# Contiguous loads, 32x32 vector transposes and one Silu in a fused attention and MoE kernel

## The chip, the cores and the metric

The kernel runs on one core of one Trainium2 chip. The time is device microseconds (us) of that core. Engines are named as in the profile: PE is TensorE (matmuls), PEld its weight loads, DVE is VectorE, ACT is ScalarE, POOL is GpSimd, SP is SyncE, which here issues DMAs. A run is called slow when it is more than 1.5% above the fastest run of the same kernel. Most slow runs of this case go with a lower mean granted TensorE clock (not all: the slow run of `a_short` has 0.95, as two of its fast ones have), and comparisons here use fast runs only, unless said otherwise. The profile's span is about 2 us shorter than the device time of the same run.

## The reference

There are B=4 batches, H=4 heads, S=1088 tokens, D=32 and sketch rank r=8. Each row of q and k becomes 64 features, the products of 8 numbers `a` and 8 numbers `b`. The result of attention is the input x (4352 tokens by 128) of a mixture layer with 2048 hidden units.

```python
def phi(x):                                   # x: q or k, (4, 4, 1088, 32)
    a = einsum('rd,bhsd->bhsr', S1, x)        # 8 numbers a token
    b = einsum('rd,bhsd->bhsr', S2, x)        # 8 more
    return outer(a, b).reshape(..., 64)
kv  = einsum('bhsf,bhsd->bhfd', phi(k), v)
z   = phi(k).sum(axis=2)
num = einsum('bhsf,bhfd->bhsd', phi(q), kv)
den = einsum('bhsf,bhf->bhs', phi(q), z)[..., None] + 1e-6
x   = (num / den).transpose(0, 2, 1, 3).reshape(4352, 128)
h   = x @ w_in                                # 128 -> 2048
g   = h * sigmoid(beta * h)
out = g @ w_out                               # 2048 -> 128, float32
```

Both kernels fold beta into the weights (`winp = w_in * beta`, `woutp = w_out / beta`), so that g is a plain `h * sigmoid(h)`, which is Silu.

## The kernel before

Attention runs a batch at a time. Between its steps the program puts in "waves" of the mixture layer: a wave is two blocks of 128 hidden units for 512 tokens. The parts that matter here are these; cuts are marked.

```python
# loads: one DMA per head, in pieces of D*4 = 128 bytes; q, k on SP, v and weights on Pool
eng.dma_start(out=dst, in_=bass.AP(tensor=bh.tensor, offset=bh.offset,
                                   ap=[[D, P], [P * D, NSUB], [1, D]]))
# ... q4, k4 turned to qT4, kT4 by 128x128 fp32 transposes on PE, copied out by ACT ...

# a and b of q and k: abps -> abT; then a is spread to 64 rows by DMA:
nc.sync.dma_start(out=arep[64 * m : 64 * m + 64, :],
                  in_=bass.AP(tensor=asrc.tensor, offset=asrc.offset,
                              ap=[list(asrc.ap[0]), [0, R], [1, S]]))
# b is spread by a PE product with s2e, and phi(q) is their product on DVE:
nc.tensor.matmul(out=brep[:, :cw], lhsT=s2e[...], rhs=qT4[...], start=True, stop=True)
nc.vector.tensor_tensor(out=qp[...], in0=arep[...], in1=brep[:, :cw], op=mult)
# ... k: abT transposed (tkps), kp4all = a*b on DVE, transposed again (stage, kpt),
#     zcol = reduce_sum(kpt) on DVE, kvz = kp^T v on PE, assembled as ndb by ACT ...

# num and den in one PE product; the divide:
nc.scalar.activation(out=deps[...], in_=ndp[64:128, :cw], func=Identity, bias=epsb[...])
nc.vector.reciprocal(out=deps[:, :cw], in_=deps[:, :cw])
for pi in range(2):
    nc.vector.tensor_tensor(out=xT[...], in0=ndps[pi][0:64, :cw], in1=deps[...], op=mult)

# a wave: PE, then sigmoid on ACT, then a multiply on DVE that reads PSUM again
nc.scalar.activation(out=sig[:, :, :tw], in_=wave[:, :, :tw], func=Sigmoid)
nc.vector.tensor_tensor(out=gT[:, w0i : w0i + 2, :tw], in0=wave[:, :, :tw],
                        in1=sig[:, :, :tw], op=mult)
# ... end of a chunk: outT_ps over 16 blocks, copied by ACT, transposed on PE, copied, stored ...
```

Of the kernel before, what the change touches and what calls it, by code (L numbers as in the profile page):

```python
# [9 lines left out]
F16 = mybir.dt.float16  # L11

P = 128
# [3 lines left out]
def kernel(  # L17
# [20 lines left out]
    assert DM == H * D  # L38
    NP2 = 2

    s_sub = []
    o = 0
    while o < S:
        s_sub.append((o, min(P, S - o)))
        o += P
    NSUB = len(s_sub)
    s_chk = []
    o = 0
    while o < S:
        s_chk.append((o, min(512, S - o)))  # L50
        o += 512
    TCH = 512
    tok_chk = []
    o = 0
    while o < NTOK:
        tok_chk.append((o, min(TCH, NTOK - o)))
        o += TCH

    const = ctx.enter_context(tc.tile_pool(name="const", bufs=1))

    ident = const.tile([P, P], F32, tag="ident")
    make_identity(nc, ident)

    scat = const.tile([P, H * 2 * R], F32, tag="scat")
    nc.vector.memset(scat, 0.0)
    s2e = const.tile([P, P], F32, tag="s2e")
    nc.vector.memset(s2e, 0.0)
    with nc.allow_non_contiguous_dma(reason="tiny sketch-matrix transposes"):
        for h in range(H):
            nc.sync.dma_start(  # L70
                out=scat[32 * h : 32 * h + 32, 16 * h : 16 * h + 8],
                in_=S1.rearrange("r d -> d r"),
            )
            nc.sync.dma_start(
                out=scat[32 * h : 32 * h + 32, 16 * h + 8 : 16 * h + 16],
                in_=S2.rearrange("r d -> d r"),
            )
    for pi in range(NP2):
        for m in range(2):
            h = 2 * pi + m  # L80
            dst = s2e[64 * pi + 32 * m : 64 * pi + 32 * m + 32, 64 * m : 64 * m + 64]
            dst3 = bass.AP(tensor=dst.tensor, offset=dst.offset, ap=[[dst.ap[0][0], 32], [R, R], [1, R]])
            srcb = scat[32 * h : 32 * h + 32, 16 * h + 8 : 16 * h + 16]
            src3 = bass.AP(tensor=srcb.tensor, offset=srcb.offset, ap=[[srcb.ap[0][0], 32], [0, R], [1, R]])
            nc.vector.tensor_copy(out=dst3, in_=src3)

    xT = const.tile([P, NTOK], F16, tag="xT")
    epsb = const.tile([P, 1], F32, tag="epsb")
    nc.vector.memset(epsb, 1e-6)

    sbA = ctx.enter_context(tc.tile_pool(name="sbA", bufs=2))
    sbB = ctx.enter_context(tc.tile_pool(name="sbB", bufs=2))
    sbC = ctx.enter_context(tc.tile_pool(name="sbC", bufs=4))
    sbD = ctx.enter_context(tc.tile_pool(name="sbD", bufs=3))
# [4 lines left out]
    vcol = [0, 32, 65, 97]  # L99

    def load_batch(b):
        q4 = sbA.tile([P, NSUB, H, D], F32, tag="q4")
        k4 = sbA.tile([P, NSUB, H, D], F32, tag="k4")
        v4 = sbA.tile([P, NSUB, 130], F32, tag="v4")
        for h in range(H):
            for srcT, dst, eng in (
                (q, q4[:, :, h, :], nc.sync),
                (k, k4[:, :, h, :], nc.sync),
                (v, v4[:, :, vcol[h] : vcol[h] + D], nc.gpsimd),
            ):  # L110
                bh = srcT[b, h]
                if b == B - 1 and h == H - 1:
                    eng.dma_start(
                        out=dst[:, : NSUB - 1, :],
                        in_=bh[: (NSUB - 1) * P].rearrange("(t p) d -> p t d", p=P),
                    )
                    eng.dma_start(
                        out=dst[: S - (NSUB - 1) * P, NSUB - 1, :],
                        in_=bh[(NSUB - 1) * P :],
                    )  # L120
                else:
                    eng.dma_start(  # L122
                        out=dst,
                        in_=bass.AP(
                            tensor=bh.tensor,
                            offset=bh.offset,
                            ap=[[D, P], [P * D, NSUB], [1, D]],
                        ),
                    )
        nc.vector.memset(v4[:, :, 64:65], 1.0)  # L130
        nc.vector.memset(v4[:, :, 129:130], 1.0)
        return q4, k4, v4

    loaded = {0: load_batch(0)}
# [3 lines left out]
    NJH = NJ // 2  # L138
    if True:
        wstage = const  # L140
        beta_bc = wstage.tile([P, DFF], F32, tag="beta_bc")
        nc.gpsimd.dma_start(
            out=beta_bc,
            in_=bass.AP(tensor=moe_beta.tensor, offset=moe_beta.offset, ap=[[0, P], [1, DFF]]),
        )
        for half in range(2):
            w_in_sb = wstage.tile([P, DFF // 2], F32, tag="w_in_sb")
            nc.gpsimd.dma_start(out=w_in_sb, in_=moe_w_in[:, half * (DFF // 2) : (half + 1) * (DFF // 2)])
            nc.vector.tensor_tensor(
                out=winp[:, half * (DFF // 2) : (half + 1) * (DFF // 2)],  # L150
                in0=w_in_sb,
                in1=beta_bc[:, half * (DFF // 2) : (half + 1) * (DFF // 2)],
                op=mybir.AluOpType.mult,
            )
        betat = wstage.tile([P, NJ], F32, tag="betat")
        with nc.allow_non_contiguous_dma(reason="strided beta gather (one time)"):
            nc.sync.dma_start(out=betat, in_=moe_beta.rearrange("(j p) -> p j", p=P))
        rbetat = wstage.tile([P, NJ], F32, tag="rbetat")
        nc.vector.reciprocal(out=rbetat, in_=betat)
        for half in range(2):  # L160
            w_out_sb = wstage.tile([P, NJH, P], F32, tag="w_out_sb")
            nc.gpsimd.dma_start(
                out=w_out_sb,
                in_=moe_w_out[half * NJH * P : (half + 1) * NJH * P, :].rearrange("(j p) m -> p j m", p=P),
            )
            nc.vector.tensor_tensor(
                out=woutp[:, half * NJH : (half + 1) * NJH, :],
                in0=w_out_sb,
                in1=bass.AP(
                    tensor=rbetat.tensor,  # L170
                    offset=rbetat.offset + half * NJH,
                    ap=[[rbetat.ap[0][0], P], [1, NJH], [0, P]],
                ),
                op=mybir.AluOpType.mult,
            )

    moe_state = {"ci": 0, "w": 0, "gT": None, "ready_tokens": 0}

    def _moe_chunk_waves(ci, w0, nwaves):
        t0, tw = tok_chk[ci]  # L180
        gT = moe_state["gT"]
        for wi in range(nwaves):
            w0i = w0 + 2 * wi
            wave = psm.tile([P, 2, TCH], F32, tag="wave")
            for jj in range(2):
                jg = w0i + jj
                nc.tensor.matmul(  # L187
                    out=wave[:, jj, :tw],
                    lhsT=winp[:, jg * P : (jg + 1) * P],
                    rhs=xT[:, t0 : t0 + tw],  # L190
                    start=True,
                    stop=True,
                )
            sig = sbB.tile([P, 2, TCH], F16, tag="sig")
            nc.scalar.activation(  # L195
                out=sig[:, :, :tw],
                in_=wave[:, :, :tw],
                func=mybir.ActivationFunctionType.Sigmoid,
            )
            nc.vector.tensor_tensor(  # L200
                out=gT[:, w0i : w0i + 2, :tw],
                in0=wave[:, :, :tw],
                in1=sig[:, :, :tw],
                op=mybir.AluOpType.mult,
            )

    def _moe_chunk_tail(ci):
        t0, tw = tok_chk[ci]
        gT = moe_state["gT"]
        outT_ps = pso.tile([P, TCH], F32, tag="moeout")  # L210
        for j in range(NJ):
            nc.tensor.matmul(  # L212
                out=outT_ps[:, :tw],
                lhsT=woutp[:, j, :],
                rhs=gT[:, j, :tw],
                start=(j == 0),
                stop=(j == NJ - 1),
            )
        outT_sb = sbB.tile([P, TCH], F32, tag="outT_sb")
        nc.scalar.copy(out=outT_sb[:, :tw], in_=outT_ps[:, :tw])  # L220
        nsubt = (tw + P - 1) // P
        out_sb = sbB.tile([P, TCH // P, P], F32, tag="out_sb")
        otok = pso.tile([P, TCH], F32, tag="moeout")
        for u in range(nsubt):
            uw = min(P, tw - u * P)
            nc.tensor.matmul(
                out=otok[:uw, u * P : u * P + P],
                lhsT=outT_sb[:, u * P : u * P + uw],
                rhs=ident,
# [232 lines left out]
```

## Time and profile before

The median of the first three runs was 311.13 us (308.25 to 314.45). The table divides the span by the ends of the last xT write of a batch, which is where a batch of attention is finished.

| stretch of the span (310.9 us) | us | what runs |
|---|---|---|
| start to the end of batch 0 | 96.3 | attention alone |
| batches 1 to 3 | 180.0 | attention with waves between its steps |
| the tail | 34.6 | waves alone |

These lines are from the page of the kernel before: busy time by engine, the busy tenths of PE and the granted TensorE clock in 40 equal slices, the DMA packets, and the chain of work that ended last by engine.

```profile
PE 198.6 (64%) x790; PEld 105.6 (34%) x790; DVE 161.6 (52%) x204; ACT 127.5 (41%) x216; POOL 20.8 (7%) x28
...
PE   0007302698559929994696499668927995686762
...
PEclk9999855555557967998779579975985899789998
...
DMA packets 48939, 17.04 MB, mean 55 GB/s; under 512 B 42144, under 2 KB 46752, under 8 KB 48800
...
PE 38%; DVE 19%; DMA 15%; SPq 14%; ACT 9%; issue 3%; ACTq 0%; DVEq 0%
```

No engine is full, and PE does almost nothing in the first three slices. The chain spends 29% of the span on DMA transfers and on SP issuing them. The next lines are the costly groups of the same page. After the bar stand the busy time and the mean ns of one; after the second bar stand the idle time just before them and what ended most of it.

```profile
L200 DVE TENSOR_TENSOR gT<-wave,sig 128x1024 f16<-128x1024 f32 (+1 forms) x72 | 81.9, 1154 | 38.9 <-ACT sig L195 38.5
L195 ACT ACTIVATE sig<-wave 128x1024 f16<-128x1024 f32 (+1 forms) x72 | 69.2, 978 | 46.4 <-PE wave L187 43.5
...
L321 DVE TENSOR_TENSOR qp<-arep,brep 128x512 f32<-128x512 f32 (+1 forms) x24 | 11.3, 527 | 46.7 <-DMA arep<-abT 46.7
L419 DVE RECIPROCAL deps<-deps 128x512 f32<-128x512 f32 (+1 forms) x12 | 29.0, 2413 | 7.9 <-ACT deps L412 7.9
```

The multiply of the waves takes half of DVE's work, and phi(q) waited 46.7 us for the DMA that spreads a. Whether such waits count is seen in the chain of waits, in order of time (start, length, what):

```profile
45.12 12.25 DMA arep<-abT
60.49 3.12 PE stage L370 x9
63.61 4.22 PE kvz L384 x18
...
102.79 11.36 DMA arep<-abT
```

They count: the arep copy is on the chain in every batch, for 12.25 us in the first and about 11.4 us in each other. The ACT and DVE timeline of the tail shows why a wave is slow when nothing else runs:

```profile
278.64 2.16 ACT L195 ACTIVATE sig<-wave 128x1024 f16<-128x1024 f32 x2 [0.98 <-PE wave L187]
...
279.70 2.36 DVE L200 TENSOR_TENSOR gT<-wave,sig 128x1024 f16<-128x1024 f32 x2 [0.61 <-ACT sig L195]
...
281.60 2.16 ACT L195 ACTIVATE sig<-wave 128x1024 f16<-128x1024 f32 x2 [0.81 <-PE wave L187]
```

A pair of waves comes every 281.60 - 278.64 = 2.96 us. The wave's PSUM buffer is held by sigmoid and then by the multiply, so ACT idles 0.8 to 1 us in each pair.

### The profile page before, as it was taken

To read this page: it belongs to the slowest core of one execution; us is meant where nothing else is said; L and a number is where in the kernel's file an instruction comes from. 1 tells how busy PE (TensorE), PEld (TensorE's weight loads), DVE (VectorE), ACT (ScalarE), POOL (GpSimd) and SP (SyncE) were. 2 spreads that over 40 slices of the span, in tenths; PEclk is the share of its full clock that TensorE was granted. 3 is DMA by queue.
4 is the path that set the end of the run, shared out by engine and by line. 5 is a ranking of instruction groups with operands and counts; after the bars stand their busy time and mean duration, and the time that the engine had idled before them with its cause. 6 is when DMAs were issued, how large, how long until landed. Compare 5 with 4: busy or idle time off the path is not lost.

```text
span 310.9 us, 2305 instructions
## 1 busy us (share of the span) xinstructions
PE 198.6 (64%) x790; PEld 105.6 (34%) x790; DVE 161.6 (52%) x204; ACT 127.5 (41%) x216; POOL 20.8 (7%) x28
## 2 busy tenths in 40 slices
PE   0007302698559929994696499668927995686762
PEld 0005101386125314641442148225403571242231
DVE  1003301421676336858933376786325849887862
ACT  1003000132157415572563064735630755377762
POOL 8202200004100000050000000000000000000000
PEclk9999855555557967998779579975985899789998
DMA  4999954811203745030104410001142100010110
GB/s 74 296 146 122 219 71 91 124 17 30 47 0 50 81 82 103 13 75 0 34 2 54 82 41 2 0 0 34 16 61 67 37 0 0 0 34 2 34 34 18
DMA packets 48939, 17.04 MB, mean 55 GB/s; under 512 B 42144, under 2 KB 46752, under 8 KB 48800
## 3 DMA queue, kind: packets, MB, share of 16 engines
q1 hardware_dynamic: 42672, 9.18, 21.6%
q0 software_dynamic: 1760, 5.50, 6.7%
q10 hardware_dynamic: 4496, 2.23, 2.6%
q8 instruction: 6, 0.10, 0.1%
q14 instruction: 5, 0.04, 0.0%
HBM read 10.22 MB, written 2.23 MB: 40 GB/s over the span
## 4 chain that ended last, share of the span: by engine, by line
PE 38%; DVE 19%; DMA 15%; SPq 14%; ACT 9%; issue 3%; ACTq 0%; DVEq 0%
DMA arep<-abT 15%; SPq L122 10%; DVE gT L200 9%; DVE deps L419 9%; PE kvz L384 7%; PE wave L187 6%; PE ndp L405 5%; ACT sig L195 5%; PE stage L370 5%; PE outT_ps L212 4%; PE brep L314 4%; PE stage L274 3%; SPq L303 2%; PE abps L289 2%; ACT deps L412 2%
## 5 line engine op out<-in xcount | busy, mean ns | idle before, releaser
L200 DVE TENSOR_TENSOR gT<-wave,sig 128x1024 f16<-128x1024 f32 (+1 forms) x72 | 81.9, 1154 | 38.9 <-ACT sig L195 38.5
L195 ACT ACTIVATE sig<-wave 128x1024 f16<-128x1024 f32 (+1 forms) x72 | 69.2, 978 | 46.4 <-PE wave L187 43.5
L187 PE MATMUL wave<-xT,winp 128*128 128x512 f16 (+1 forms) x144 | 50.5, 426 | 21.3 <-DVE gT L200 20.5
L212 PE MATMUL outT_ps<-gT,woutp 128*128 128x512 f16 (+1 forms) x144 | 46.1, 408 | 13.3 <-DVE gT L200 12.1
L321 DVE TENSOR_TENSOR qp<-arep,brep 128x512 f32<-128x512 f32 (+1 forms) x24 | 11.3, 527 | 46.7 <-DMA arep<-abT 46.7
L419 DVE RECIPROCAL deps<-deps 128x512 f32<-128x512 f32 (+1 forms) x12 | 29.0, 2413 | 7.9 <-ACT deps L412 7.9
L405 PE MATMUL ndp<-qp,ndb 128*128 128x512 f32 (+1 forms) x48 | 26.3, 675 | 5.6 <-DVE xT L421 3.9
L187 PEld LDWEIGHTS <-winp 128*128 128x128 f16 x144 | 16.1, 114 | 31.6 <-issue 24.9
L412 ACT ACTIVATE deps<-ndp,epsb 64x512 f32<-64x512 f32 (+1 forms) x24 | 13.4, 559 | 30.1 <-PE ndp L405 29.9
L212 PEld LDWEIGHTS <-woutp 128*128 128x128 f16 x144 | 14.9, 106 | 27.2 <-issue 17.6
L405 PEld LDWEIGHTS ndp<-qp,ndb 128*128 128x128 f32 x48 | 11.2, 261 | 34.5 <-DVE xT L421 18.1
L274 PE MATMUL stage<-ident,q_103 128*128 128x128 f32 (+1 forms) x9 | 2.2, 418 | 25.3 <-DMA q_103<-in_q_dram 25.3
L314 PE MATMUL brep<-qT_157,s2e 64*128 64x512 f32 (+1 forms) x12 | 6.2, 672 | 18.5 <-DVE qp L321 18.5
L370 PE MATMUL stage<-ident,kp4all 128*128 128x128 f32 (+1 forms) x72 | 16.2, 324 | 1.2 <-DVE kp4all L360 1.0
L381 DVE TENSOR_REDUCE zcol<-kpt 128x1 f32<-128x1088 f32 x8 | 10.2, 1279 | 11.1 <-ACT kpt L379 11.1
L345 ACT COPY tkS<-tkps 128x512 f32<-128x512 f32 (+1 forms) x8 | 2.9, 400 | 28.2 <-PE tkps L335 28.1
L360 DVE TENSOR_TENSOR kp4all<-tkS 128x256 f32<-128x256 f32 (+1 forms) x36 | 12.4, 417 | 1.8 <-ACT tkS L345 1.8
L370 PEld LDWEIGHTS stage<-ident,kp4all 128*128 128x128 f32 (+1 forms) x72 | 10.0, 155 | 8.3 <-DVE kp4all L360 5.8
L421 DVE TENSOR_TENSOR xT<-ndp,deps 64x512 f16<-64x512 f32 (+1 forms) x24 | 12.5, 523 | 0.5
L379 ACT COPY kpt<-stage 128x512 f32<-128x512 f32 (+1 forms) x24 | 10.3, 463 | 5.2 <-PE stage L370 5.0
L220 ACT COPY outT_sb<-outT_ps 128x512 f32<-128x512 f32 (+1 forms) x9 | 5.0, 560 | 17.7 <-PE outT_ps L212 17.7
L283 ACT COPY qT_157<-stage 128x512 f32<-128x512 f32 (+1 forms) x3 | 1.3, 463 | 24.7 <-PE stage L274 24.7
(96 smaller groups left out, 199.5 us busy)
## 6 DMA issues: line engine op xcount, KB each, us to landing
arep<-abT SPq DMA_DIRECT2D x16, 272.0 KB
out_dram<-out_sb ACTq DMA_DIRECT2D x8, 256.0 KB, 2.3
beta_bc<-in_moe_beta_dram POOLq DMA_DIRECT2D x1, 1024.0 KB, 9.0
w_in_sb<-in_moe_w_in_dram POOLq DMA_DIRECT2D x2, 512.0 KB, 7.8
w_out_sb<-in_moe_w_out_dram POOLq DMA_DIRECT2D x2, 512.0 KB, 9.4
q_103<-in_q_dram SPq DMA_DIRECT2D x4, 144.0 KB
v_105<-in_v_dram POOLq DMA_DIRECT2D x4, 144.0 KB, 5.1
k_104<-in_k_dram SPq DMA_DIRECT2D x4, 144.0 KB, 11.9
```

The source lines that it names most:

```text
L122: eng.dma_start(out=dst, in_=bass.AP(tensor=bh.tensor, offset=bh.offset, ap=[[D, P], [P * D, NSUB], [1, D]],),)
L187: nc.tensor.matmul(out=wave[:, jj, :tw], lhsT=winp[:, jg * P : (jg + 1) * P], rhs=xT[:, t0 : t0 + tw], start=True, stop=True,)
L195: nc.scalar.activation(out=sig[:, :, :tw], in_=wave[:, :, :tw], func=mybir.ActivationFunctionType.Sigmoid,)
L200: nc.vector.tensor_tensor(out=gT[:, w0i : w0i + 2, :tw], in0=wave[:, :, :tw], in1=sig[:, :, :tw], op=mybir.AluOpType.mult,)
L212: nc.tensor.matmul(out=outT_ps[:, :tw], lhsT=woutp[:, j, :], rhs=gT[:, j, :tw], start=(j == 0), stop=(j == NJ - 1),)
L314: nc.tensor.matmul(out=brep[:, :cw], lhsT=s2e[64 * pi : 64 * pi + 64, :], rhs=qT4[64 * pi : 64 * pi + 64, c0 : c0 + cw], start=True, stop= ...
L370: nc.tensor.matmul(out=stage[:, gi * P : gi * P + sw], lhsT=kp4[g0 + gi][:sw, pi * P : (pi + 1) * P], rhs=ident[:sw, :sw], is_transpose=Tr ...
L384: nc.tensor.matmul(out=kvz[:, 0:65], lhsT=kp4[st][:sw, pi * P : (pi + 1) * P], rhs=v4[:sw, st, pi * 65 : pi * 65 + 65], start=(st == 0), s ...
L405: nc.tensor.matmul(out=ndp[:, :cw], lhsT=ndblk[pi], rhs=qpT[pi][:, c0 : c0 + cw], start=True, stop=True,)
L412: nc.scalar.activation(out=deps[64 * pi : 64 * pi + 64, :cw], in_=ndp[64:128, :cw], func=mybir.ActivationFunctionType.Identity, bias=epsb[ ...
L419: nc.vector.reciprocal(out=deps[:, :cw], in_=deps[:, :cw])
L421: nc.vector.tensor_tensor(out=xT[64 * pi : 64 * pi + 64, b * S + c0 : b * S + c0 + cw], in0=ndps[pi][0:64, :cw], in1=deps[64 * pi : 64 * p ...
```

## The change

The intent is to shorten every one of these stages: load q and k in runs of 34 tokens (4352 bytes), turn them with DVE transposes of 32x32 blocks instead of PE transposes, spread a by a PE product instead of a DMA, compute k's features already transposed for the kv sums in 32-column tiles of PE, divide num by den in one 128-row operation, replace sigmoid and multiply by one Silu, and transpose the output straight out of PSUM. The token order inside a head is permuted by the loads, and the stores undo it. The core of the diff, with cuts:

```diff
-    eng.dma_start(out=dst, in_=bass.AP(..., ap=[[D, P], [P * D, NSUB], [1, D]]))   # per head; v on Pool
+    nc.sync.dma_start(out=t, in_=bass.AP(tensor=src.tensor, offset=src[b, 0].offset,
+                                         ap=[[T * D, P], [1, T * D]]))    # a whole batch, T = 34
+    # order on SP: k0, v0, q0, w_in, w_out, then k, v, q of batches 1 to 3; S1, S2, beta on ACT
-    # PE transposes into `stage`, ACT copies to qT4, kT4
+    nc.vector.transpose(out=kT, in_=k_t[b].rearrange("p t d -> p (t d)"))
+    # a and b of k, by 32x32 tiles, then turned out of PSUM:
+    nc.tensor.matmul(out=kps[32 * g : 32 * g + 32, : NJK * 32], lhsT=sw[rows, :], rhs=kT[...])
+    nc.vector.transpose(out=kab[:, h]..., in_=kps[:, : NJK * 32])
+    # kp = a*b: heads 0, 1 on DVE, heads 2, 3 on Pool
-    nc.sync.dma_start(out=arep[64 * m : 64 * m + 64, :], in_=...)          # spread a by DMA
+    nc.tensor.matmul(out=aps[:, :cw], lhsT=sa[rows, :], rhs=qT[rows, c0 : c0 + cw])
+    nc.scalar.copy(out=asb[pi][:, :cw], in_=aps[:, :cw])                   # spread a by PE
-    # kpt transposes, reduce_sum zcol, kvz of 18 matmuls
+    for n, j in enumerate([1, 2, 3, 4, 5, 6, 7, 8, 0]):                    # kv and z sums
+        for which in range(2):
+            for h in range(H):
+                nc.tensor.matmul(out=kvz[32 * h : 32 * h + 32, F * which : F * which + F],
+                                 lhsT=v_t[b][:kr, h, j, :] if which == 0 else ones[:kr, :],
+                                 rhs=kp[:kr, h, j, :], ...)
-    for pi in range(NP2): nc.vector.tensor_tensor(out=xT[64 * pi ...], ...)
+    nc.vector.tensor_tensor(out=xT[:, ...], in0=num[:, :cw], in1=deps[:, :cw], op=MUL)
-    nc.scalar.activation(out=sig, in_=wave, func=Sigmoid)
-    nc.vector.tensor_tensor(out=gT, in0=wave, in1=sig, op=mult)
+    nc.scalar.activation(out=g, in_=wv, func=ACTF.Silu)
-    # ACT copy, PE transposes, ACT copy, store
+    nc.vector.transpose(out=o_sb..., in_=moe["acc"][:, :tw])               # then store, 128-byte pieces
+    # beta is spread by PE (ones_row x beta_row -> bb) instead of a broadcast DMA
+    for b in range(B):
+        steps = attention(b)
+        if b == 0:
+            next(steps)
+            next(steps)
+            prep_weights()
+        for _ in steps:
+            pump(2)                       # two waves after each of the nine steps, where ready
```

## The prediction

> **What bounds the kernel now.** No engine is full: the profile's first part has PE 64%, DVE 52%, ACT 41%. Time goes in three stretches (chain of waits and a table of stretches). (a) 0 to 92 us: one batch of attention alone. PE first works at 25.3 us, because q and k arrive as 128-byte pieces (42,144 of 48,939 packets are under 512 B; the chain gives 10% to issuing those loads); the arep copies hold qp from 45 to 57 us; then PE runs at a granted clock of 0.5. (b) 92 to 272 us: three batches of about 60 us, each with an 11.4 us wait of qp for arep (46.7 us of waits in all) and the long chain of kp transposes, zcol, kvz and ndb. (c) 272 to 311 us: MoE alone. A wave is read by both sigmoid (1.03 us) and the DVE multiply (1.21 us), so with two wave buffers a pair of waves takes 2.96 us (timeline).
>
> **What changes.**
> - ACT: 72 Sigmoids become 68 Silus. I take 1.03 us each: the Trainium skill, "ScalarE: Activation LUTs" (step-by-step section), says one element per cycle whatever the function; the trace's 1026 and 598 ns for 1024 and 512 elements fit that rate. Out and q/k evictions go. Estimate: 127 to about 93 us.
> - DVE: 82 us of gT multiplies go; 33 transposes of estimated 0.45 to 1.3 us come (about 23 us). The reciprocal keeps its 29 us (6.3 ns an element, from 3348 and 544 ns), xT halves. 162 to about 85 us.
> - PE: about 90 fp32 transposes go; kps, doubled a/b products and 288 small kvz matmuls come. fp32 costs 0.85 us per 512 columns at full clock, double at half (the same six brep records took 2.15 us at 31 us and 4.10 at 52 us). Column tiles do overlap here: the two abps matmuls start within 10 ns. This agrees with the skill's "TensorE: Matmul & The Clock Gate", Part 3. So per batch I estimate kps 2.5, a/b 6, kvz 7 (144 passes near 50 ns, the shakiest term), num/den 4: 20 us, plus 16 waves at 0.86 us = 14: 34 us, the fullest engine.
> - DMA: arep (4.4 MB) and the beta broadcast vanish; q/k/v load in long runs. Output is now in 128-byte pieces, but off the chain until the last.
>
> **Sum.** First kps near 8 us instead of 25. Batch 0 ends at about 44 us (w_in landing, partly a cold clock, three 3.1 us reciprocal/xT steps); three batches of about 41 us (PE 34 plus stalls: three PSUM banks let the reciprocal chain of about 9 us hold num/den and, in program order, the waves behind them); then 20 waves left, ACT-bound at 1.05, 21 us, plus 4 for the last transpose and store: 44 + 123 + 25 = 192 us. Nearly all of the 119 us gain lies on the chain: about 48 from the start, 57 from the batches, 14 from the tail.
>
> I predict 192 us, 8 in 10 between 170 and 218; faster by over 2% 0.98, within 2% 0.01, slower 0.01.
>
> **What would show it.** First PE work at 7 to 12 us; no arep waits; Silu mean near 1.03 us; tail spacing about 1.05 us a wave with ACT over 90% there; stretches of about 41 us between the batches' last xT writes; PE the busiest engine; deps reciprocal the longest DVE group.
>
> **What would make it wrong.** kvz passes not overlapping or paying more for weight loads or tile changes (over 12 us a batch); a half clock throughout attention (plus 30 us); Pool products (kp, woutp) slow enough to hold kvz; evictions queued behind Silu on ACT making PE wait. Faster if a/b row pairs overlap and the clock stays full (170).

## The result

The changed kernel gives the right output. Its median is 182.31 us over four runs (181.04 to 188.35), beside 310.2 us for the kernel before in the same rounds (308.25 to 314.45). One run of each was slow. The ratio of the fast runs is 0.5875, with a 95% interval of 0.5835 to 0.5916. A ratio here is always the mean time of one kernel's fast runs over that of the other's of the same rounds, so it is not quite the ratio of the medians quoted. A later control of the unchanged new kernel on another chip (`a_again`, below) gave 182.3 us.

| stretch | before | after | predicted |
|---|---|---|---|
| start to the end of batch 0 | 96.3 | 44.7 | 44 |
| batches 1 to 3 | 180.0 | 112.1 | 123 |
| tail | 34.6 | 23.4 | 25 |
| sum | 310.9 | 180.2 | 192 |

So 51.6 us of the gain lie in the start, 67.9 in the batches and 11.2 in the tail. The same lines of the page as before:

```profile
PE 147.1 (82%) x1201; PEld 59.9 (33%) x1201; DVE 82.0 (45%) x113; ACT 88.9 (49%) x122; POOL 15.0 (8%) x17
...
PE   0079996849999998399999977999999738988870
...
PEclk9999999699999999969999999999999995799998
...
DMA packets 22480, 11.35 MB, mean 63 GB/s; under 512 B 18738, under 2 KB 20802, under 8 KB 22338
...
PE 68%; ACT 9%; DVE 9%; issue 7%; DMA 4%; ACTq 0%; SPq 0%; DVEq 0%
```

PE now starts in the third slice and holds 68% of the chain; DMA and its issue have fallen from 29% to 4%. The groups that answer to those shown before:

```profile
L228 ACT ACTIVATE g<-wave 128x1024 f16<-128x1024 f32 x68 | 66.2, 1021 | 28.9 <-PE wave L220 28.7
...
L359 DVE RECIPROCAL deps<-deps 128x384 f32<-128x384 f32 (+1 forms) x12 | 28.4, 2395 | 7.0 <-ACT deps L358 7.0
...
L304 DVE TENSOR_TENSOR qp<-bps,asb 128x384 f32<-128x384 f32 (+1 forms) x24 | 12.4, 533 | 30.2 <-PE bps L301 30.0
```

A Silu of 1024 elements took 1021 ns and the sigmoid that it replaces 1026 ns. This agrees with the Trainium skill, "ScalarE: Activation LUTs", section "Step-by-step: what each stage is for", which says that the throughput is one element per cycle and lane whatever the function, measured there as 0.833 ns an element. Here the difference between sigmoids of 1024 and 512 elements gives (1026 - 598) / 512 = 0.836 ns.

The reciprocal kept its cost (28.4 us against 29.0). The idle time before phi(q) is still 30 us, but it is now waiting for PE, the fullest engine, and is no cost in itself.

The table of stretches of the changed kernel (window, its length, busy time and instructions of PE, PEld, DVE, ACT and POOL, then granted clock, DMA share, GB/s), for the start from 10 us on, the three batches, and the tail:

```profile
10.00:44.70 34.70, 29.34 (x248) 13.18 (x225) 25.10 (x31) 9.66 (x22) 6.43 (x3) 0.95 0.69 202
44.70:82.00 37.30, 33.24 (x297) 12.72 (x296) 19.26 (x26) 19.84 (x27) 2.73 (x2) 0.95 0.10 15
82.00:119.00 37.00, 34.97 (x302) 13.46 (x299) 17.63 (x25) 22.68 (x30) 2.31 (x2) 1.00 0.10 15
119.00:156.00 37.00, 32.32 (x275) 12.26 (x274) 15.52 (x20) 18.91 (x27) 2.31 (x2) 0.91 0.10 16
156.00:180.20 24.20, 16.84 (x85) 8.04 (x84) 2.38 (x4) 16.18 (x17) 0.00 (x0) 0.98 0.18 28
```

PE is busy for 33.24 of 37.3 us in the first batch, 34.97 and 32.32 of 37.0 in the next two. In the tail's timeline, ACT is the limit:

```profile
159.49 1.94 ACT L228 ACTIVATE g<-wave 128x1024 f16<-128x1024 f32 x2 [0.26 <-PE wave L220]
161.68 1.94 ACT L228 ACTIVATE g<-wave 128x1024 f16<-128x1024 f32 x2 [0.26 <-PE wave L220]
```

A pair of waves now comes every 161.68 - 159.49 = 2.19 us, 1.10 us a wave instead of 1.48, and ACT idles 0.26 us of each pair.

### The profile page after: what moved, and what is told of

The parts are those of the page before. It is cut to its first block, busy times and chain, and to the rows that moved or that the text cites. A ratio compares the mean times of both kernels' runs of the same rounds, so it can differ in the third digit from the quotient of the medians.

```text
span 180.2 us, 2944 instructions
## 1 busy us (share of the span) xinstructions
PE 147.1 (82%) x1201; PEld 59.9 (33%) x1201; DVE 82.0 (45%) x113; ACT 88.9 (49%) x122; POOL 15.0 (8%) x17
## 2 busy tenths in 40 slices
DMA packets 22480, 11.35 MB, mean 63 GB/s; under 512 B 18738, under 2 KB 20802, under 8 KB 22338
## 4 chain that ended last, share of the span: by engine, by line
PE 68%; ACT 9%; DVE 9%; issue 7%; DMA 4%; ACTq 0%; SPq 0%; DVEq 0%
PE wave L220 17%; PE moeout L180 16%; PE aps L293 10%; ACT g L228 7%; PE kvz L314 6%; PE bps L301 5%; PE kps L261 5%; DVE deps L359 4%; PE bb L152 4%; PE num L350 3%; DMA v<-in_v_dram 3%; PE den L350 2%; DMA sraw<-in_S_dram 1%; ACT deps L358 1%; DVE xT L360 1%
## 5 line engine op out<-in xcount | busy, mean ns | idle before, releaser
L228 ACT ACTIVATE g<-wave 128x1024 f16<-128x1024 f32 x68 | 66.2, 1021 | 28.9 <-PE wave L220 28.7
L180 PE MATMUL moeout<-g,woutp 128*128 128x512 f16 (+1 forms) x144 | 41.9, 375 | 4.0 <-ACT g L228 4.0
L359 DVE RECIPROCAL deps<-deps 128x384 f32<-128x384 f32 (+1 forms) x12 | 28.4, 2395 | 7.0 <-ACT deps L358 7.0
L304 DVE TENSOR_TENSOR qp<-bps,asb 128x384 f32<-128x384 f32 (+1 forms) x24 | 12.4, 533 | 30.2 <-PE bps L301 30.0
L293 PE MATMUL aps<-qT,sa 64*128 64x384 f32 (+1 forms) x48 | 22.0, 581 | 0.1
L180 PEld LDWEIGHTS <-woutp 128*128 128x128 f16 x144 | 12.1, 98 | 26.7 <-issue 17.7
L297 ACT COPY asb<-aps 128x384 f32<-128x384 f32 (+1 forms) x24 | 11.2, 465 | 17.6 <-PE aps L293 12.8
L277 POOL TENSOR_TENSOR kp<-kab 128x576 f32<-128x576 f32 x8 | 10.2, 1291 | 105.8 <-DVE kab L268 105.8
L350 PE MATMUL num<-qp,nd 128*64 128x384 f32 (+1 forms) x48 | 13.8, 535 | 5.7 <-DVE xT L360 5.7
L301 PE MATMUL bps<-qT,sb 64*128 64x384 f32 (+1 forms) x48 | 16.5, 544 | 0.0
L350 PE MATMUL den<-qp,nd 128*64 128x384 f32 (+1 forms) x48 | 10.7, 525 | 1.3 <-DVE nd L343 1.2
```

The source lines that it names most:

```text
L180: nc.tensor.matmul(out=moe["acc"][:, :tw], lhsT=woutp[:, j, :], rhs=g[:, jj, :tw], start=(j == 0), stop=(j == NJ - 1),)
L228: nc.scalar.activation(out=g, in_=wv, func=ACTF.Silu)
L277: eng.tensor_tensor(out=kp[:, h].rearrange("p j (i l) -> p j i l", i=R), in0=bass.AP(tensor=a0.tensor, offset=a0.offset, ap=[pst, [32, NJK ...
L293: nc.tensor.matmul(out=aps[:, :cw], lhsT=sa[rows, :], rhs=qT[rows, c0 : c0 + cw], start=True, stop=True)
L297: nc.scalar.copy(out=asb[pi][:, :cw], in_=aps[:, :cw])
L301: nc.tensor.matmul(out=bps[:, :cw], lhsT=sb[rows, :], rhs=qT[rows, c0 : c0 + cw], start=True, stop=True)
```

## The experiments

Twelve kernels ran. The first four build parts of the change into the kernel before, to see what each is worth there. The rest take parts out of the changed kernel, or change one thing in it. The theories were these. Theory A (the prediction): the gain comes from removing chain items one by one (late loads, arep, DVE multiply), and what is left is bound by PE in the batches. Its rivals: one single item explains most of it; the piece size of the loads explains the start; PE is not the limit, but the reciprocal's chain is.

The stretches of the runs that the argument uses, from their profiles, cut as above (all of fast runs):

| kernel | start to end of batch 0 | batches 1 to 3 | tail | span |
|---|---|---|---|---|
| before | 96.3 | 180.0 | 34.6 | 310.9 |
| `b_silu` | 96.1 | 165.4 | 20.9 | 282.4 |
| `b_aps` | 78.1 | 145.7 | 45.6 | 269.4 |
| `b_aps_silu` | 77.2 | 125.6 | 22.3 | 225.1 |
| `b_order` | 68.3 | 125.6 | 22.8 | 216.6 |
| after | 44.7 | 112.1 | 23.4 | 180.2 |
| `a_kvz` | 51.2 | 130.5 | 23.4 | 205.1 |
| `a_f16ab` | 43.4 | 96.5 | 23.4 | 163.3 |
| `a_pump` | 44.9 | 97.9 | 24.9 | 167.7 |
| `a_final` | 40.3 | 97.6 | 24.9 | 162.8 |

### Silu alone in the kernel before: `b_silu`

```diff
-            nc.scalar.activation(out=sig[:, :, :tw], in_=wave[:, :, :tw], func=Sigmoid)
-            nc.vector.tensor_tensor(out=gT[...], in0=wave[:, :, :tw], in1=sig[:, :, :tw], op=mult)
+            nc.scalar.activation(out=gT[...], in_=wave[:, :, :tw], func=Silu)
```

> The kernel before with Silu written straight to gT, no DVE multiply. Theory (the gain comes from the chain: load pieces, arep copies and the long attention chain; the MoE counts only in the tail): the tail of 39 us falls by about 10, each 60 us batch by at most 3, so 290 to 300 us. Rival (the costliest group, the 82 us gT multiply on DVE, was what bounded the kernel): at most 245 us.

Measured: 283.5 us (282.4 to 285.0), ratio 0.916 (0.910 to 0.922), a gain of about 26.5 us. That is more than the theory allowed (290 to 300 us) and far less than the rival asked (245 us or less). DVE's busy time fell from 161.6 to 83.3 us, so only a third of the 78 us taken from DVE came off the time. The list of waits of this run says where the rest went (who waited for what, us in total, times, longest):

```profile
DVE qp L314 <- DMA arep<-abT: 89.8, 8, 18.6
```

DVE now arrives earlier at phi(q) and waits there for the arep DMA, 89.8 us instead of 46.7. The gain is 13.7 us in the tail, where waves run alone, and 14.6 in the batches.

### The spread of a by PE alone, in the kernel before: `b_aps`

```diff
-                nc.sync.dma_start(out=arep[64 * m : 64 * m + 64, :], in_=bass.AP(... [0, R] ...))
+            for c0, cw in s_chk:
+                aps = ps.tile([P, 512], F32, tag="bank")
+                nc.tensor.matmul(out=aps[:, :cw], lhsT=s1e[64 * pi : 64 * pi + 64, :],
+                                 rhs=qT4[64 * pi : 64 * pi + 64, c0 : c0 + cw], start=True, stop=True)
+                nc.scalar.copy(out=arep[:, c0 : c0 + cw], in_=aps[:, :cw])
```

> The kernel before with arep made by a PE product and an ACT copy instead of the DMA copies. Theory: the 46.7 us of waits for arep go, some 2 to 4 us of PE work per batch comes, 262 to 278 us. Rival (DVE multiply the bound): at least 300 us, since the multiplies would fill the time.

Measured: 271.1 us (270.6 to 271.8), ratio 0.876 (0.871 to 0.881), a gain of 39 us, less than the 46.7 us of waits removed. The start and the batches gained 18.2 and 34.3 us, but the tail grew by 11 us. The table of stretches for this tail:

```profile
224.00:269.40 45.40, 29.33 (x130) 12.59 (x128) 30.93 (x29) 28.48 (x36) 0.00 (x0) 0.95 0.07 20
```

28 sigmoids start after the last batch here, and 21 in the kernel before: attention now ends sooner, and the waves, which still need sigmoid and multiply, have not kept up.

### Both together: `b_aps_silu`

The edit is the sum of the two above.

> Both single changes in the kernel before. Theory: gains add, 245 to 265 us, and the rest of the way to 182 is the loads, transposes and kp/kvz chain. Rival: with the arep wait gone the DVE multiply matters far more than alone: 215 us or less.

Measured: 227.15 us (226.8 to 228.3), ratio 0.7345 (0.730 to 0.739), a gain of 83 us. The two gains alone sum to 26.5 + 39 = 65.5, so together they give about 17 us more. Neither expectation was met: the gains do not just add (245 to 265 us), and the rival's 215 us was not reached. In the profiles the excess is 85.8 - 28.5 - 41.5 = 15.8 us, and the stretches place it: 9.6 us in the tail (which grew by 11.0 with the PE spread alone and shrinks by 12.3 with both), 5.5 in the batches, 0.7 in the start. Each fix alone ran into the wait that the other removes. The table of stretches over the three batches, first of the kernel before, then of this one, shows the same from the side of PE:

```profile
96.70:276.30 179.60, 135.86 (x561) 70.77 (x559) 110.20 (x129) 88.23 (x152) 4.48 (x5) 0.83 0.21 36
```

```profile
77.20:202.80 125.60, 118.87 (x594) 65.10 (x593) 57.74 (x83) 92.23 (x170) 4.46 (x5) 1.00 0.13 27
```

PE is now busy for 118.87 of 125.6 us, and its granted clock in this stretch rose from 0.83 to 1.00. Two of the many edits, neither touching transposes or loads, explain 83 of the 128 us.

### The order of the loads: `b_order`

`b_aps_silu` with all loads on the one SP queue in the order of need; the pieces stay 128 bytes. Each half of w_in and w_out also gets a tile of its own, so that no load waits for a tile to come free.

```diff
-                (v, v4[:, :, vcol[h] : vcol[h] + D], nc.gpsimd),
+                (v, v4[:, :, vcol[h] : vcol[h] + D], nc.sync),
-        nc.gpsimd.dma_start(out=beta_bc, ...)      # w_in, w_out likewise
+        nc.sync.dma_start(out=beta_bc, ...)        # after q, k, v of batch 0
```

> The kernel before with both single changes (arep on PE, Silu), and all loads on one queue in the order of need: sketch matrices, q, k, v of batch 0, then the weights, then batch 1. The pieces stay 128 bytes. Theory (competition: 3 MB of weights and v on a second queue held back q and k, more than the piece size did): first PE work at 13 to 18 us instead of 25, 212 to 221 us. Rival (the number of small pieces, among them 4-byte ones for the sketch matrices, sets the start): first PE work after 22 us, 227 us within 2%.

Measured: 219.01 us (218.4 to 220.6), ratio 0.703 (0.696 to 0.710). The control of the changed kernel ran on the same chip:

> The changed kernel, unaltered, on the same chip and rounds as the next one: 182 us within 1%.

It gave 182.3 us (182.1 to 183.2), ratio 0.585. The PE timeline shows the first PE work, first in the kernel before, then in `b_order`:

```profile
25.30 1.94 PE L274 MATMUL stage<-ident,q_103 128*128 128x128 f32 x8 [25.30 <-DMA q_103<-in_q_dram]
```

```profile
16.87 2.23 PE L274 MATMUL stage<-ident,q 128*128 128x128 f32 x9 [16.87 <-DMA q<-in_q_dram]
```

PE starts 8.4 us sooner with pieces of the same size (`b_aps_silu`, the direct neighbour, starts at 25.38 us, as late as the kernel before), and the whole kernel gains about 8 us, all in the start (77.2 to 68.3). So the loads on the second queue (v, the weights and beta) had been holding q and k back. This agrees with the Trainium skill, "DMA: Bandwidth & Descriptors", section "Queues, rings and completion order", which says that each DMA engine serves the queues that have work in turn. Which of the moved loads did the harm, and whether the second queue or only the order mattered, was not separated. It was not the number of short pieces: packets under 512 B even rose, from 42,016 to 60,384.

### The piece size of the loads, undone in the changed kernel: `a_short`

```diff
-        t = ld.tile([P, T, D], F32, tag=tag, name=tag)
+        t = ld.tile([P, T, D + 8], F32, tag=tag, name=tag)      # padded rows: no long runs
-            out=t, in_=bass.AP(..., ap=[[T * D, P], [1, T * D]]))
+            out=t[:, :, :D], in_=bass.AP(..., ap=[[T * D, P], [D, T], [1, D]]))
```

> The changed kernel with k and q loaded in 128-byte pieces (same tiles, padded rows), all else kept. Theory (short pieces are what delayed the first PE work, 25.3 us before against 9.6 after): the first kps comes 4 to 12 us later, later batches do not care, 186 to 196 us. Rival (the earlier start comes from the order of the loads and the missing arep, not the piece size): within 2% of 182.

Measured: median 184.5 us, fast runs 183.2 to 184.6, ratio 0.593 (0.590 to 0.596), beside 181.9 us for the mean of the changed kernel's fast runs in its own rounds. Packets under 512 B rose from 18,738 to 53,554, and the transpose of k started at 6.73 us instead of 5.35. So short pieces cost 1.4 us at the first load and about 2 us in all. The expectation of 4 to 12 us was wrong. Little of the time hung on the piece size: the first PE work waits for the turned sketch matrices, and it moved only from 9.64 to 10.25 us. The DVE and PE timelines of `a_short`:

```profile
6.73 1.31 DVE L254 STREAM_TRANSPOSE kT<-k 128x1088 f32<-128x1088 f32 x1 [5.38 <-DMA k<-in_k_dram]
```

```profile
10.25 1.25 PE L261 MATMUL kps<-kT,sw 32*32 32x288 f32 x24 [10.25 <-DVE sw L119]
```

### Sigmoid and multiply put back: `a_sigmoid`

```diff
-        nc.scalar.activation(out=g, in_=wv, func=ACTF.Silu)
+        sig = sbG.tile([P, 2 * TCH], F16, tag="sig", name="sig", bufs=2)
+        nc.scalar.activation(out=sig, in_=wv, func=ACTF.Sigmoid)
+        nc.vector.tensor_tensor(out=g, in0=wv, in1=sig, op=MUL)
```

> The changed kernel with Sigmoid and a DVE multiply in place of Silu. Theory: the tail grows by about 9 us (a pair of waves back to about 2.96 us), the batches from 37 to about 43 because DVE then has 40 us of work each: 205 to 220 us. Rival (Silu is most of the gain): 245 us or more.

Measured: one fast run of 202.94 us; three others (206.6 to 210.1), with the profiled one among them, count as slow, so no ratio was formed. The fast run lies 2 us below the expected 205 to 220. Fast against fast, Silu is worth about 202.9 - 181.9 = 21 us in the changed kernel. With a single fast run this is a rough number. In the kernel before it was 26.5 alone and, on top of the PE spread, 271.1 - 227.15 = 44. The worth of one edit depends on what else is in place.

### The order of heads in the kv sums: `a_kvz`

The matmuls are the same in number and shape, but the loop over heads is outermost, so that neighbours write to the same 32 output rows of PSUM, that is, to the same column tile of PE.

```diff
-        for n, j in enumerate([1, 2, 3, 4, 5, 6, 7, 8, 0]):
-            kr = 64 if j == 0 else P
-            for which in range(2):
-                for h in range(H):
+        for h in range(H):
+            for n, j in enumerate([1, 2, 3, 4, 5, 6, 7, 8, 0]):
+                kr = 64 if j == 0 else P
+                for which in range(2):
```

> The changed kernel with the loop over heads outside in kvz, so that neighbouring small matmuls use the same 32-column tile. Theory (column tiles overlap, which is why kvz took 2.2 us and not the 7 of the prediction): kvz 6 to 9 us a batch, 195 to 208 us in all. Rival (a pass costs its 16 ns of issue wherever it goes): kvz stays near 2.2 us, 182 us.

Measured: 208.84 us (207.2 to 210.1), ratio 0.674 (0.670 to 0.679), about 27 us slower. From the chain of waits, first the changed kernel, then `a_kvz` (start, length, what):

```profile
27.84 2.37 PE kvz L314 x144
...
63.94 2.16 PE kvz L314 x134
```

```profile
27.72 8.98 PE kvz L314 x144
...
70.43 8.74 PE kvz L314 x140
```

A record (each fp32 matmul leaves two) takes 8.74 / 140 = 62 ns in this order and 2.16 / 134 = 16 ns when the four heads alternate, about four times less. The product takes 6 to 9 us, as the theory expected; the total is a little above its 195 to 208. The difference of 6.6 us a batch, four times, is 26.4 us, which is about the whole loss. The PE timeline of the changed kernel shows the same from closer by (start, time from first start to last end, group):

```profile
27.82 0.32 PE L314 MATMUL kvz<-kp,v 128*32 128x64 f32 x8
27.95 0.29 PE L314 MATMUL kvz<-kp,ones 128*32 128x64 f32 x8
```

A group of eight records lasts about 0.3 us, and the next group starts 0.12 to 0.13 us after it began. This agrees with the Trainium skill, "TensorE: Matmul & The Clock Gate", Part 3 ("Packing small matmuls"), which says that matmuls in different tiles of the array run at the same time and start about 4 ns apart. The 4 ns are not shown here: the trace gives 16 ns a record on average. The new order also changes which weights follow each other and which rows of PSUM are written in turn; no run separates these from the column tile.

### a and b of q in half precision: `a_f16ab`

Its output is wrong, which doesn't matter for the time. `sa`, `sb` and a copy of qT made on Pool are float16, so the 96 records of those products become 48.

```diff
-    sa = const.tile([P, P], F32, tag="sa")      # sb likewise
+    sa = const.tile([P, P], F16, tag="sa")
+        nc.gpsimd.tensor_copy(out=qTh, in_=qT)  # qTh float16, used as rhs of aps and bps
```

> The changed kernel with the a and b products in float16 (qT cast on the idle Pool; the result may be off, and is only to show time). Theory (PE bounds the batches): PE loses 5 us or more a batch, 160 to 168 us. Rival (evictions behind Silu on ACT and three PSUM banks set the pace of this stretch): within 2% of 182, with PE idle in its place.

Measured: fast runs 165.1 and 163.3 us. PE's busy time fell by 17.3 us (147.1 to 129.8), and the mean of the fast runs by 181.9 - 164.2 = 17.7. The batches gained 15.6 of it and the tail nothing. So PE is what binds the batches of the changed kernel, as predicted: a microsecond taken from PE there came off the time.

### Waves dealt evenly: `a_pump`

PE binds, but it is not always busy. The changed kernel puts two waves after every step while the layer has tokens ready. In the first of these batches 16 waves are ready, and they are all spent before the divide begins. In the table of stretches of the changed kernel, the end of batch 1 looks like this, and ACT's timeline below it shows no wave from 69.4 to 79.1 us:

```profile
69.70:82.30 12.60, 9.46 (x46) 3.03 (x46) 9.40 (x9) 3.62 (x5) 0.00 (x0) 0.86 0.14 21
```

```profile
68.34 1.02 ACT L228 ACTIVATE g<-wave 128x1024 f16<-128x1024 f32 x1
70.63 0.58 ACT L358 ACTIVATE deps<-den,epsb 128x384 f32<-128x384 f32 x1 [1.27 <-PE den L350]
71.92 0.58 ACT L358 ACTIVATE deps<-den,epsb 128x384 f32<-128x384 f32 x1 [0.71 <-PE den L350]
76.71 0.53 ACT L358 ACTIVATE deps<-den,epsb 128x320 f32<-128x320 f32 x1 [4.21 <-DVE xT L360]
79.07 1.94 ACT L228 ACTIVATE g<-wave 128x1024 f16<-128x1024 f32 x2 [1.83 <-PE wave L220]
```

DVE works through the reciprocals, and PE has nothing to fill the time with: it stands idle for 3.15 us from 73.5 us on. The wait costs twice, for the work that follows runs at a granted clock of 0.51. A finer cut of the same table:

```profile
76.60:79.80 3.20, 3.12 (x7) 0.77 (x7) 3.14 (x4) 1.26 (x2) 0.00 (x0) 0.51 0.31 45
```

The experiment spreads the waves:

```diff
-        for _ in steps:
-            pump(2)
+        for i, _ in enumerate(steps):
+            pump(1 if b == 0 or i < 6 else (4, 4, 2)[i - 6])
```

> The changed kernel with the MoE waves dealt out more evenly: one at each early step of a batch, four beside each of the first two reciprocal steps. Theory (in the reciprocal stretch, about 11 us a batch, PE and ACT stand idle some 4 to 6 us because all waves ready were spent earlier): 166 to 176 us. Rival (PE is full, so waves are only moved): within 2% of 182.

Measured: the output is right; fast runs 169.8 and 168.4 us, two slow ones of 174.0 and 175.3; ratio 0.5447 (0.5406 to 0.5488), about 13 us faster than the changed kernel. The stretch with the reciprocals of batch 1 in this run:

```profile
64.00:78.10 14.10, 14.06 (x74) 4.54 (x74) 9.38 (x8) 9.72 (x13) 0.00 (x0) 1.00 0.12 18
```

PE is busy for 14.06 of 14.10 us, beside the same 9.4 us of DVE work. Over the three batches of `a_pump` (44.9 to 143 us) PE is idle for 0.7 us a batch, where it was idle for 3.6 in the changed kernel, and its busy time is 32.0 us a batch instead of 33.5; the granted clock is 1.00 in all three, where it was 0.95, 1.00 and 0.91. The rival theory, that the reciprocal's chain sets the batch, holds only where the program leaves PE without other work.

### Moving the beta products: `a_best`

In the changed kernel the eight records that spread beta (`bb`) hold PE for 7.19 us in the first batch, before the first `aps`. PE's timeline there:

```profile
9.64 1.25 PE L261 MATMUL kps<-kT,sw 32*32 32x288 f32 x24 [9.64 <-DVE sw L119]
11.43 1.18 PE L261 MATMUL kps<-kT,sw 32*32 32x288 f32 x8 [0.55 <-DVE kab L268]
12.62 7.19 PE L152 MATMUL bb<-beta_row,ones_row 1*128 1x512 f32 x8
```

This kernel is `a_pump` with half of the small loads of S1 and S2 moved to Pool's queue, and with the beta products after the first num and den.

```diff
-        nc.scalar.dma_start(out=sraw[32 * g + R : 32 * g + 2 * R, :], in_=S2)
+        nc.gpsimd.dma_start(out=sraw[32 * g + R : 32 * g + 2 * R, :], in_=S2)
         if b == 0:
-            next(steps)
-            next(steps)
+            for _ in range(7):
+                next(steps)
             prep_weights()
```

> The changed kernel with the waves dealt out evenly (as a_pump, 168 to 170 us fast), half of the S loads issued from Pool, and the beta products for the weights (bb, 7.2 us of PE before the first aps) moved behind the first num. Theory (bb and the late S loads lie on the chain of batch 0): kps 1 to 3 us earlier, 160 to 166 us. Rival (batch 0 waits for the loads of q, w_in and v anyway): 167 us or more. Also: if a one-row bb pass takes 0.85 us because the PE is really at half clock early on, a later one takes 0.43; if it is the shape, it stays 0.85.

Measured: one fast run of 169.25 us, three slow ones (172.1 to 176.1, the profiled one among them), so no gain over `a_pump` can be read from it. The expectation was missed. PE did start earlier (kps at 7.70 us), and the first xT came at 30.56 us instead of 39.82, but the second came only at 40.57. Batch 0 ended at 41.46 us, before the 44.9 of `a_pump`; this slow run lost more than that in batch 1, where the granted clock was 0.55 from 41.5 to 50 us. The PE timeline of this (slow) run:

```profile
26.02 0.87 PE L350 MATMUL den<-qp,nd 128*64 128x384 f32 x4 [0.52 <-DVE nd L343]
...
27.46 1.98 PE L152 MATMUL bb<-beta_row,ones_row 1*128 1x512 f32 x4
...
33.05 1.55 PE L350 MATMUL den<-qp,nd 128*64 128x384 f32 x4
```

The beta products had moved from in front of the chain into the middle of it, and the den products behind them took 1.55 us instead of 0.87. Four of the `bb` records took 1.98 us here, 0.50 each, while all eight took 7.19 us in the changed kernel, 0.90 each; so it was not their shape that made them slow there. At these rates PE ran at about half speed both in the early `bb` of the changed kernel and in the den after the moved `bb`. For that den the record agrees: the granted clock from 33 to 35 us of this run is 0.50. For the early `bb` it is inferred from the durations alone: the granted clock recorded for 12.6 to 19.8 us of the changed kernel is 1.00. The Trainium skill, "TensorE: Matmul & The Clock Gate", Part 1, says that half speed is the default, that some 3.4 us of sustained activity release it, and that the clock records of a trace can be unreliable. The last agrees with the record of 1.00 beside halved products; the release after 3.4 us did not come in the first 10 us of nearly unbroken PE work of the changed kernel, most of it on a single row of the array. That one-row products do not count as activity is a guess that no run tests.

### The best version: `a_final`

`a_pump` with the same change of the small loads, beta spread by a broadcast DMA behind w_in, `winp` made on Pool, and no `bb` on PE.

```diff
-    nc.scalar.dma_start(out=beta_row, in_=moe_beta.rearrange("(o f) -> o f", o=1))
+    nc.sync.dma_start(out=beta_bc, in_=bass.AP(..., ap=[[0, P], [1, DFF]]))
-        for c in range(0, DFF, 512): ...        # bb on PE, winp on DVE
+        nc.gpsimd.tensor_tensor(out=winp, in0=w_in_sb, in1=beta_bc, op=MUL)
```

> The changed kernel with the waves dealt out evenly, half of the S loads issued from Pool, and no bb products at all: beta comes in by a broadcast load and Pool makes winp. a_best lost its early gain again because bb then sat between num and den, with the PE back at half clock for the den and num after it. Theory (bb is chain time of batch 0 wherever it stands on PE): batch 0's last xT ends at 37 to 40 us instead of 44.7, 160 to 165 us in a fast run. Rival (batch 0 is paced by the reciprocals and the half clock, bb was hidden): 167 us or more.

Measured: the output is right. The median of six runs is 167.75 us; the fast ones are 164.58 and 164.13, the other four lie between 167.7 and 168.5 and count as slow. The kernel before took 310.4 us (median) in the same rounds, so its fast runs are at about 164.4 / 310 = 0.53 of it. Compared with `a_pump`'s fast runs (mean 169.1, on another chip) it gains about 5 us, 4.6 of them in the start (44.9 to 40.3, just above the expected 37 to 40). The small loads and `bb` were changed together here; the first kps comes 0.8 us earlier (8.82 us), the rest of the 4.6 us lies behind it. It is the best of all versions with a right output.

## Why the prediction was right, and where it was off

- **The total.** 192 us were predicted, with 170 to 218 as the range, and 182.3 us were measured: inside the range, 5% below the middle. The chance of 0.98 for faster was borne out.
- **The start.** The end of batch 0 was predicted at 44 us and came at 44.7. That the number fits so well is in part luck: the `bb` products do not stand in the prediction's list of PE work, and without them, and with earlier small loads, `a_final` ends batch 0 at 40.3. The first PE work was predicted near 8 us and came at 9.64. But the reason given for the old start, "because q and k arrive as 128-byte pieces", was the wrong step. With pieces still short, a better order of the loads brought the first PE work forward by 8.4 us (`b_order`), and with short pieces put back into the changed kernel it moved by only 0.6 us (`a_short`). What held q and k back were the loads on the other queue.
- **arep.** Its waits went, and were worth 39 us alone, as expected from a wait on the chain. That this gain and Silu's would add up to more than their sum was not foreseen: the prediction summed stages and not edits, and so was not hurt by it.
- **The batches.** 41 us each were predicted, PE work of 34 and stalls of 7, and 37.4 on average measured. The term that was mis-sized is the stalls. PE was busy for 33.24, 34.97 and 32.32 us in the three stretches shown above, 33.5 on average, and idle for 4.06, 2.03 and 4.68, or 3.6 on average. So the sum of 34 us of PE work was met, but by errors that cancel, and that is luck. In "kps 2.5, a/b 6, kvz 7 (144 passes near 50 ns, the shakiest term), num/den 4", kvz took 2.2 us and not 7, because alternating column tiles brought a record to 16 ns; `a_kvz`, at 62 ns, shows that 50 ns would have been near the truth without overlap. Counted from start to start in PE's timeline, with its idle time left out, kps took about 1.9 us, a/b 6.9, num/den 5.2 and the waves 16.3 instead of 14: what kvz saved went to the others, in part because PE ran at half clock after it had stood idle. `a_pump`, which only deals out the waves, brought a batch to 32.7 us, 32.0 of them PE work.
- **The tail.** 25 us predicted, 23.4 measured. A wave takes 1.10 us, not 1.05, and 16 were left, not 20; after the last Silu (174.89 us) 5.3 us went by, not 4. ACT is busy for 1.94 of 2.19 us in a pair of waves, 89%, a little under the 90% expected.
- **Engines.** ACT was predicted at 93 us and measured at 88.9, DVE at 85 and 82.0. The prediction does not say what its "0.45 to 1.3 us" for a DVE transpose was worked out from; the trace has 0.47 us for 288 elements a row, 0.70 for 512 and 1.30 for 1088. PE became the fullest engine, and `a_f16ab` shows that it binds the batches.
- **Feared and not seen.** "A half clock throughout attention" did not happen in the batches, where the recorded clock is 0.91 to 1.00 over a batch, though 0.51 for the 3.2 us after PE's idle time shown above. In the first 20 us it seems to have happened without the record saying so.

What stays open: the last 37 us between `b_order` (219.0) and the changed kernel (182.3) come from the new k path, the DVE transposes, the single xT operation and the early small loads together. The stretches place 23.6 us of them in the start (7.2 of these in the earlier first PE work, 16.87 to 9.64) and 13.5 in the batches; the piece size is worth about 2 us, and the rest was not separated by edit. `a_sigmoid` and `a_best` have one fast run each.

## What to carry to other kernels

Read for each stage which wait ends last, and expect two fixes in one stage to be worth more, or less, than their sum: here 26.5 and 39 us became 83, because each alone only moved the work to the other's wait. When one engine has become the limit, look for stretches in which it is idle for lack of filler, and keep the independent work for those; dealing the same waves out evenly gave 13 us for two lines, and PE's granted clock then stayed at 1.00 through the batches. Small fp32 products are cheap when neighbours in program order use different column tiles, four times dearer when they do not; and the order of loads over queues can matter more than the length of their pieces.

## What the Trainium skill lacked or had wrong

- "VectorE: DVE Perf Modes" says that reciprocal is an iterative divide with a repeat count of 8, but no page has its duration. Here it took 2395 ns on average for 320 to 384 elements a row, and 3348 ns for 512 against 544 ns for 64, which is 6.3 ns an element, and 28 us in the whole kernel.
- "TensorE: Matmul & The Clock Gate", Part 1, has half speed released by about 3.4 us of sustained activity. Here eight one-row products took 7.19 us between 12.6 and 19.8 us, after 3 us of other PE work, at 1.8 times the time per record that they took in another run (1.98 us for four), while the recorded clock was 1.00. The page's warning on unreliable clock records fits; it has nothing on products that use one row.
- The same page, Part 3, lists measured gains for three column tiles but none for four with short products. Here four alternating column tiles of 64-column fp32 products took 16 ns a record, against 62 ns with the same tile back to back.
- "DMA: Bandwidth & Descriptors", section "Specifications", gives 512 bytes as the least piece for line rate, and the page has no measured time of HBM loads in 128-byte pieces on trn2. Here 128-byte pieces for q and k delayed the first load by 1.4 us and the kernel by about 2 us, much less than loads on a competing queue (8.4 us at the first PE work).
